# Attention, top-1 experts and a gated MLP on one core: gate values through TensorE, another order in the routing and in the first expert, four weight splits on GpSimd

## The chip, the cores and the metric

One core of a Trainium2 chip runs the whole program. The metric is the device time of one execution in microseconds (us); less is better. The engines are TensorE (PE; its weight loads are a row of their own, PEld), VectorE (DVE), ScalarE (ACT), GpSimd (POOL) and SyncE (SP). SP issues nearly all DMAs, POOL issues the DMAs that gather rows by index. Each engine works through its own queue in order and waits on semaphores.

## What is computed

Attention over 2 x 8 heads of 576 tokens and 64 columns, with the scores under (row maximum - tau) masked out; its output is a matrix `x` of 1152 rows and 512 columns. Each row goes to one of 8 experts:

```python
logits = x @ w_gate                       # 1152 x 8
expert_idx = np.argmax(logits, axis=1)
gate_w = softmax(logits)[arange, expert_idx]
h = relu(x_rows_of_e @ w1[e])             # 512 -> 1024
y = h @ w2[e]                             # 1024 -> 512
out[i] = gate_w[i] * y[row i]             # rows beyond the capacity: 0
# then: (silu(out @ w_gate2) * (out @ w_val)) @ w_out, 512 -> 1536 -> 512
```

## The kernel before

**Stages.** Attention runs to about 163 us, the routing to 174 us, the eight experts to about 300 us, the gated MLP to the end at 543 us. Work on the experts uses products in fp32r, in which each operand is a high part plus a low remainder; so each weight buffer is split in "pieces" of 128 x 1024: ScalarE writes the high part (`split_hi`, L220), VectorE subtracts it from the raw weights for the low part (L300). A ring of six pieces holds them. `next_piece` emits the split of the next piece; for VectorE the subtraction is put off to the call of `next_piece` that follows (`late`). `next_raw` lets SP load the next 1 MB of weights (four for each expert) when a raw buffer is free.

**Routing** (L1060 to L1230). From the logits VectorE makes a one-hot `oh`, the gate value `gs`, and counts `osb` for each partition. TensorE sums the counts over all partitions (`ps_c`), and makes each token's position inside its expert (prefix sums: `p0_` for the first expert, `pt_` for all). The experts are ordered by size: `key`, `krow` and `gc` come from the counts, and `pt_` is finished with `gc` (L1150). VectorE then derives the sorted place `dst` of each token, one-hot rows `olo`, and TensorE turns them into `ids`, the token of each sorted place. `info` holds the order of the experts, `slack` the number on which every engine branches to one of several programs; the one that runs here is the one for a smallest expert with at most 64 tokens ("packed").

**First expert.** Its rows are not gathered: `pick_rows` multiplies the rows by one-hot columns `hot` on TensorE (nine tiles of 128 tokens, eight short matmuls by two for each), and the sum `ps_x0` becomes `x0`.

**Other experts.** Every row of `x` lies in DRAM in `xd`, with its gate value as column 513 (`put_gates`, L1074: two DMAs of ScalarE, two of SP). POOL gathers the rows in sorted order, 128 to a tile (`gather`, L1290; the first three L1216). VectorE multiplies a tile by its gate column (`sort_scale`, L1304), TensorE transposes it (`sort_tile`, L1313, four matmuls), ScalarE copies it to `xsT` (L1322). `window(e)` takes an expert's columns out of `xsT`.

**Order.** All of this is a hand-written order of emission. `SORTP` is a table of ones and zeros: at which step of which expert a tile is sorted. `expert_first` runs the first expert: four products with `w1` (L1491), a turn of the result (`turn`, a fold on TensorE and two copies), four products with `w2`, and after each of these eight steps one call of `next_piece`. `expert_rows` does the same for the second and third (L1417, six matmuls a product).

Of the kernel before, what the change touches and what calls it, by code (L numbers as in the profile page):

```python
# [23 lines left out]
def attention_moe_swiglu_kernel(  # L24
# [35 lines left out]
    PK = 64  # L60
# [49 lines left out]
    AOLO = (5,)  # L110
    VH, PH, AH = (8,0), (1,2,3,4), (5,6,7)
# [15 lines left out]
    olo_all = const.tile([128, NTL, 128], F16, name="olo")  # L127
    olo = [olo_all[:, t] for t in range(NTL)]
    rhs = const.tile([128, NTL, NTL], F16, name="rhs")
    x0 = const.tile([128, KD, 2 * PK], F32R, name="x0")  # L130
# [146 lines left out]
    def next_piece(lo_eng=None, hi_eng=None):  # L277
        while late:
            late.pop()()
        if used["piece"] >= len(porder):  # L280
            return
# [3 lines left out]
        pr = ring[(used["piece"] + 2) % NRING]  # L285
        if nm in ("w1", "w2"):
# [782 lines left out]
    sqw = [rt_(f"sqw{i}", [128, 128], BF16) for i in range(len(AOLO))]  # L1069
# [4 lines left out]
    def put_gates():  # L1074
        gs = xr[NP - 1][:, :, 128]
        V.reciprocal(out=gs, in_=gsum)
        for b in range(B):
            nc.scalar.dma_start(
                xd[b * S:b * S + SM, DM:DM + 1].rearrange("(p c) d -> p (c d)", c=C4),
                gs[:, b * C4:(b + 1) * C4])  # L1080
            nc.sync.dma_start(xd[b * S + SM:(b + 1) * S, DM:DM + 1],
                              gs[b * ST:(b + 1) * ST, B * C4:NTL])

    def gate_ops():
        yield lambda: V.tensor_reduce(out=gsum, in_=pexp, axis=AX.X, op=ALU.add)
        yield lambda: V.tensor_scalar(out=gsum, in0=gsum, scalar1=1e-9, scalar2=None, op0=ALU.add)
        yield put_gates
# [23 lines left out]
    cols, rows_ = [(o0, ones), (o1, ones), (ot, ones)], [(ones, o0), (ones, o1), (ones, ot)]  # L1111
    for a, (l, r_) in enumerate(cols):
        mm(ps_c[0:NE, 0:1], l, r_[:, 0:1], start=a == 0, stop=a == 2)
    for a, (l, r_) in enumerate(rows_):
        mm(ps_c[0:NE, NE:2 * NE], l[:, 0:NE], r_, start=a == 0, stop=a == 2)
    pt_ = ps_r[:, 0:NTL * NE].rearrange("p (t e) -> p t e", t=NTL)
    M4 = B * C4

    p0_ = ps_c[:, 4 * NE:4 * NE + NTL]
    prefix = [(0, C4, upper, o0), (C4, NTL, ones, o0), (C4, M4, lowh, ot), (C4, M4, upper, o1),  # L1120
              (M4, NTL, upper, ot), (M4, NTL, highc, o1)]
    for i, (a, z, l, r_) in enumerate(prefix):
# [9 lines left out]
    mm(p0_[:, 0:M4], same, pre3[:, :, 0], start=False, stop=True)  # L1132
    for i, (a, z, l, r_) in enumerate(prefix):
        mm(pt_[:, a:z], l, r_.unsqueeze(1).to_broadcast([128, z - a, NE]), start=i == 0, stop=False)
    mm(pt_[:, 0:M4], same, pre3, start=False, stop=False)
    V.tensor_scalar(out=npos, in0=p0_, scalar1=-1.0, scalar2=None, op0=ALU.mult)

    def hot_v(t):
        V.tensor_scalar(out=hot[:, t], in0=iot[:, 0:PK], scalar1=npos[:, t:t + 1],
                        scalar2=gm[:, t:t + 1], op0=ALU.is_equal, op1=ALU.mult)  # L1140

    for t in VH[:1]:
        hot_v(t)
# [17 lines left out]
    hord = [VH[0], VH[1], PH[0], AH[0], PH[1], PH[2], AH[1], PH[3], AH[2]]  # L1161
# [11 lines left out]
    keep_warm(mp, WA[1])  # L1173
# [594 lines left out]
```

## Time and profile before

| | us |
|---|---|
| median of three runs | 545.84 (545.61 to 547.84) |
| the profiled execution | 544.49 |
| its span, first to last instruction | 542.7 |
| TensorE busy in the span | 525.4 (97%) |
| VectorE, ScalarE, GpSimd busy | 400.2, 296.6, 119.2 |

TensorE is the engine to read: from about 192 us to the end it has no gap, and its granted clock is at the full level (1.00) throughout. A row of the timeline gives start, duration, engine, line, operation, output and inputs, and in brackets the idle time before it with the instruction that ended it. TensorE's durations are modelled and overlap; the distance between two starts is the better measure.

### The profile page before, as it was taken

Reading aid. Unit: us, or ns where it says so; the run is one execution under the profiler, and the core shown is the slowest. Engines: PE = TensorE matmul, PEld = TensorE weight load, DVE = VectorE, ACT = ScalarE, POOL = GpSimd, SP = SyncE. Lnnn points to the kernel's source line nnn. Section 1 sums busy time; section 2 is a strip of 40 time slices with the busy share of each in tenths; the row PEclk is TensorE's granted clock in tenths of the full one; section 3 lists DMA queues with packets and bytes.
Section 4 is the critical chain, followed back from the end, with each engine's and each line's share of the span. In section 5 each row is a group of like instructions: output and inputs, shape, how many; then the busy total and the mean of one; then the engine's idle time right before and its main releaser. Section 6 shows DMA issues by size and latency. Waiting matters only on the chain. (4 is left out here: it accounts for less than half of the span.)

```text
span 542.7 us, 9898 instructions
## 1 busy us (share of the span) xinstructions
PE 525.4 (97%) x3648; PEld 474.2 (87%) x3648; DVE 400.2 (74%) x802; ACT 296.6 (55%) x571; POOL 119.2 (22%) x204
## 2 busy tenths in 40 slices
PE   7999999999998899999999999999999999999995
PEld 6778788888786588999999999999999999888884
DVE  6988989889966789988888968888885858622220
ACT  5986776767645699877777424234242224323221
POOL 6685292495644310000000000000000000021101
PEclk8999999999999999999999999999999999999999
DMA  6736256247303999866764442443431400001001
GB/s 190 219 93 137 71 118 131 70 97 209 124 18 74 391 398 352 308 226 231 241 197 133 146 150 81 152 134 101 155 115 46 153 2 0 1 39 40 35 24 44
DMA packets 63193, 73.83 MB, mean 136 GB/s; under 512 B 22432, under 2 KB 41504, under 8 KB 63136
## 3 DMA queue, kind: packets, MB, share of 16 engines
q1 hardware_dynamic: 60496, 68.38, 40.5%
q0 software_dynamic: 1440, 4.72, 2.2%
q8 instruction: 31, 0.51, 0.4%
q14 instruction: 26, 0.21, 0.1%
q10 hardware_dynamic: 1200, 0.00, 0.1%
HBM read 63.07 MB, written 4.72 MB: 125 GB/s over the span
## 5 line engine op out<-in xcount | busy, mean ns | idle before, releaser
L1668 PE MATMUL pgv<-yT,ring 128*128 128x384 f32 x828 | 145.3, 337 | 0.0
L1668 PEld LDWEIGHTS pgv<-yT,ring 128*128 128x128 f32 x828 | 145.1, 188 | 0.0
L1721 POOL DMA_INDIRECT out_dram<-ob,ids x9 | 10.1, 1119 | 319.1 <-ACT hs L220 270.1
L220 ACT CAST ring<-raw 128x1024 fp32r<-128x1024 f32 x48 | 51.2, 1069 | 50.2 <-DVE raw L248 48.4
L701 ACT COPY pT<-ps_pt 128x512 f32<-128x512 f32 (+1 forms) x108 | 52.3, 486 | 37.8 <-PE ps_pt L697 37.8
L675 DVE SCALAR_TENSOR_TENSOR e<-s,th,e 128x576 f32<-128x576 f32 x72 | 58.7, 815 | 5.5 <-ACT e L664 4.1
L651 DVE TENSOR_REDUCE nm<-s 128x1 f32<-128x576 f32 x72 | 54.2, 752 | 8.1 <-PE s L641 7.6
L664 ACT ACTIVATE e<-s,nm 128x576 f32<-128x576 f32 x72 | 54.3, 754 | 3.0 <-DVE nm L651 2.8
L224 DVE TENSOR_TENSOR hs<-h,hs 128x768 fp32r<-128x768 f32 x18 | 17.2, 958 | 48.1 <-ACT hs L220 48.1
L697 PE MATMUL ps_pt<-ident,e 128*128 128x128 f32 x324 | 46.9, 272 | 0.0
L220 ACT CAST ring<-rawx 128x1024 fp32r<-128x1024 f32 x28 | 29.4, 1055 | 26.0 <-DVE rawx L248 22.3
L1715 PE MATMUL po<-ring,hs 128*128 128x512 f32 x108 | 42.0, 389 | 0.0
L1716 PE MATMUL po<-ring,hs 128*128 128x512 f32 x108 | 42.0, 389 | 0.0
L1717 PE MATMUL po<-ring,hs 128*128 128x512 f32 x108 | 42.0, 389 | 0.0
L300 DVE TENSOR_TENSOR ring<-raw,ring 128x1024 fp32r<-128x1024 f32 x34 | 41.2, 1216 | 0.9 <-PE ps_h L1491 0.9
L1376 PE MATMUL ps_y<-h,ring 128*128 128x448 f32 (+3 forms) x144 | 41.5, 361 | 0.0
L719 PE MATMUL ps_pv<-pT,v 128*64 128x256 f32 (+2 forms) x400 | 40.4, 328 | 0.0
L697 PEld LDWEIGHTS ps_pt<-ident,e 128*128 128x128 f32 x324 | 39.0, 140 | 0.2 <-issue 0.2
L1377 PE MATMUL ps_y<-h,ring 128*128 128x224 f32 (+3 forms) x144 | 35.8, 248 | 0.0
L1688 ACT ACTIVATE sg<-pgv 128x384 f32<-128x384 f32 x36 | 17.6, 489 | 29.7 <-PE pgv L1668 17.8
L1689 DVE TENSOR_TENSOR h<-sg,pgv 128x384 f32<-128x384 f32 x36 | 19.6, 548 | 17.9 <-PE pgv L1668 17.5
L1376 PE MATMUL ps_h<-xw,ring 128*128 128x448 f32 (+3 forms) x112 | 32.6, 361 | 0.0
(289 smaller groups left out, 1079.8 us busy)
## 6 DMA issues: line engine op xcount, KB each, us to landing
raw<-in_moe_w_dram SPq DMA_DIRECT2D x20, 1024.0 KB, 6.0
rawx<-in_moe_w_dram SPq DMA_DIRECT2D x12, 1024.0 KB, 6.3
raw<-in_moe_w_gate_dram SPq DMA_DIRECT2D x6, 1024.0 KB, 5.8
raw<-in_moe_w_out_dram SPq DMA_DIRECT2D x5, 1024.0 KB, 4.8
raw<-in_moe_w_val_dram SPq DMA_DIRECT2D x3, 1024.0 KB, 5.1
rawx<-in_moe_w_val_dram SPq DMA_DIRECT2D x3, 1024.0 KB, 5.0
k<-in_k_dram SPq DMA_DIRECT2D x8, 256.0 KB, 3.7
q<-in_q_dram SPq DMA_DIRECT2D x8, 256.0 KB, 4.4
```

Source lines behind the costliest of these rows:

```text
L220: nc.scalar.copy(dst, src)
L300: lo_eng.tensor_tensor(out=lo_, in0=src, in1=f32(hi_), op=ALU.subtract)
L651: nc.vector.tensor_reduce(out=nm_t[u][:, j:j + 1], in_=s_t[i][:, :, 0:SH], axis=AX.XY, op=ALU.max, negate=True)
L664: nc.scalar.activation(out=e_t[u][:, j].rearrange("p (a s) -> p a s", a=2), in_=s_t[i][:, :, 0:SH], func=ACTF.Exp, bias=nm_t[u][:, j:j + 1 ...
L675: nc.vector.scalar_tensor_tensor(out=ev, in0=s_t.pop(i)[:, :, 0:SH], scalar=th_t[u][:, j:j + 1], in1=ev, op0=ALU.is_ge, op1=ALU.mult, accu ...
L697: nc.tensor.transpose(ps[:, c * 128:(c + 1) * 128], ef[:, (c0 + c) * 128:(c0 + c + 1) * 128], ident)
L701: return lambda: nc.scalar.copy(pT[g][:, c0:c0 + m, o:o + 128], ps[:, 0:m * 128].rearrange("p (c t) -> p c t", c=m))
L1376: mm(ps[:, 0:2 * W], ws(wp, 0), x[:, 0:2 * W], start=first, stop=False)
L1668: mm(ps[:, 0:TH], (gw, vw)[w][:, i, kk, fl * 128:(fl + 1) * 128], yT[:, x, kk, th * TH:(th + 1) * TH], start=i + x + kk == 0, stop=i == 1 ...
L1715: mm(po, hs[:, 0, fl], ws[:, 0, sl], start=f == 0, stop=False)
L1716: mm(po, hs[:, 0, fl], ws[:, 1, sl], start=False, stop=False)
L1717: mm(po, hs[:, 1, fl], ws[:, 0, sl], start=False, stop=f == KF2 - 1)
```

## The change

- **Gates.** `gs` stays in SBUF. The gate column of `xd`, and with it four DMAs, are dropped. Instead `gs` is split in three bfloat16 parts `gp`, multiplied into the one-hot `ohi` (`grhs`), and sorted with the same `olo` by nine more matmuls (`ps_gt`), whose sum is `gat`, the gate of each sorted place.
- **Keys ahead of prefix sums.** `key`, `krow`, `gc` come ahead of `npos` and the `hot` columns on VectorE; the prefix sums for the first expert move to another PSUM bank. The two filler matmuls ahead of `pick_rows` go.
- **`hot` and `olo`**: one `hot` column on VectorE instead of two, four on ScalarE instead of three; no `olo` on ScalarE. `ids` is made after six picked tiles, as before, but the gathers are emitted straight after it, two instead of three into the first buffer.
- **Gathers and scaling.** In the packed program a gather is emitted three tiles ahead. Tiles 2 to 8 are scaled by ScalarE. Clearing the end of `xsT` goes to POOL.
- **First expert, other order.** The subtraction of the fourth `w2` piece comes ahead of the low part of the first turn, two tiles (not three) are sorted in it, and it emits six pieces instead of eight; the other two follow in the second and third expert (`MORE`). `SORTP` sorts two tiles in each of the experts 1, 2 and 3 and one in expert 4.
- **GpSimd splits** (`POOLED`): both parts of the second and fourth `w2` piece of experts 1 and 2.

The core of the diff:

```diff
+    POOLED = tuple((e, "w2", g) for e in (1, 2) for g in (1, 3))
+    MORE = ((1, 3), (2, 3))
-    VH, PH, AH = (8,0), (1,2,3,4), (5,6,7)
+    VH, PH, AH = (8,), (0,1,2,3), (4,5,6,7)
...
+            if (e, nm, g) in POOLED and pooled:
+                lo_eng = hi_eng = nc.gpsimd
...
-    keep_warm(mp, WA[1])
     pick_rows(hord[:RT1])
...
     V.tensor_copy(out=ids, in_=ps_i[:, 0:NTL])
+    gbuf = idle.popleft()
+    first = [gbuf[:, t * DM:(t + 1) * DM] for t in range(2)]
+    for t in range(2):
+        nc.gpsimd.indirect_dma_start(first[t], None, xd[:, :],
+                                     bass.IndirectOffsetOnAxis(ap=ids[:, t:t + 1], axis=0))
+    pick_rows(hord[RT1:RT1 + 1])
...
+    V.tensor_tensor(out=gp[:, :, 0], in0=gs, in1=gs, op=ALU.max)
+    V.tensor_tensor(out=gm, in0=gs, in1=gp[:, :, 0], op=ALU.subtract)
+    V.tensor_tensor(out=gp[:, :, 1], in0=gm, in1=gm, op=ALU.max)
+    V.tensor_tensor(out=gp[:, :, 2], in0=gm, in1=gp[:, :, 1], op=ALU.subtract)
+    V.tensor_tensor(out=grhs, in0=ohi.unsqueeze(2).to_broadcast(TG),
+                    in1=gp.unsqueeze(3).to_broadcast(TG), op=ALU.mult)
...
+    for x, t in enumerate(tord):
+        mm(ps_gt[:, 0:3 * NTL], olo[t], grhs[:, t].rearrange("p v n -> p (v n)"), start=x == 0,
+           stop=x == NTL - 1)
...
+            if t < NTL and packed and t >= NG0:
+                nc.scalar.activation(out=grow[t], in_=grow[t], func=ACTF.Identity,
+                                     scale=gat[:, t:t + 1])
```

VectorE in the routing, after the counts `osb` and `pre` are made. In the changed kernel the small tiles of the routing are parts of two larger ones, so `npos` and `pos` read `spare_2453` and the `hot` columns `spare_2452`. Before:

```order
L1130 TENSOR_TENSOR pre<-pre,oh 128x2x8
L1136 TENSOR_SCALAR npos<-ps_c 128x9
L1139 TENSOR_SCALAR spare<-iot,npos,gm 128x64
L1144 TENSOR_SCALAR key<-ps_c,kcol 8x1
L1146 SCALAR_TENSOR_TENSOR krow<-ps_c,kadd 8x8
L1148 SCALAR_TENSOR_TENSOR gc<-krow,key,ps_c 8x8
L1139 TENSOR_SCALAR spare<-iot,npos,gm 128x64
L1175 TENSOR_TENSOR pos<-ps_r,oh 128x72
```

The same place in the changed kernel:

```order
L1132 TENSOR_TENSOR pre<-pre,spare_2453 128x2x8
L1140 TENSOR_SCALAR key<-ps_c,kcol 8x1
L1142 SCALAR_TENSOR_TENSOR krow<-ps_c,kadd 8x8
L1144 SCALAR_TENSOR_TENSOR gc<-krow,key,ps_c 8x8
L1157 TENSOR_SCALAR spare_2453<-ps_p 128x9
L1159 TENSOR_SCALAR spare_2452<-iot,spare_2453 128x64
L1183 TENSOR_TENSOR spare_2453<-ps_r,spare_2453 128x72
```

The three key instructions have moved ahead of `npos` and of the one `hot` column left, and `pos` follows that column.

VectorE again, from `ids` to the first instruction that follows the branch. Before:

```order
L1206 CAST ids<-ps_i 128x9
L1209 CAST info<-ps_c 3x8
L1210 TENSOR_TENSOR nd<-ps_c,wmax 1x24
L1212 TENSOR_REDUCE slack<-nd 1x3
L1226 TENSOR_TENSOR x_83<-ps_x_2549,x_83 128x2x64 x2
L1229 TENSOR_LOAD slack
```

The same place in the changed kernel:

```order
L1209 CAST ids<-ps_i 128x9
L1218 CAST info<-ps_c 3x8
L1219 TENSOR_TENSOR gp<-spare_2453 128x9
L1220 TENSOR_TENSOR spare_2453<-spare_2453,gp 128x9
L1221 TENSOR_TENSOR gp<-spare_2453 128x9
L1222 TENSOR_TENSOR gp<-spare_2453,gp 128x9
L1224 TENSOR_TENSOR grhs<-spare_2453,gp 128x243
L1226 TENSOR_TENSOR nd<-ps_c,wmax 1x24
L1228 TENSOR_REDUCE slack<-nd 1x3
L1240 TENSOR_TENSOR x_83<-ps_x_2537,x_83 128x2x64 x2
L1243 TENSOR_REDUCE gat<-ps_gt 128x9
L1245 TENSOR_LOAD slack
```

Five instructions for the gates now stand between `info` and `slack`.

POOL in the packed program, behind the branch, in the changed kernel (before, six gathers `g<-xd,ids` and nothing else stand there). The tiles `ring_97` to `ring_101` are slots of the ring of pieces, `raw` and `rawx` raw weights:

```order
L1377 MEMSET xsT 128x4x80
L1312 DMA g<-xd,ids 128x512 x4
L218 TENSOR_SCALAR ring_101<-rawx_2719 128x1024
L312 TENSOR_TENSOR ring_101<-rawx_2719,ring_101 128x1024
L218 TENSOR_SCALAR ring_97<-raw_103 128x1024
L312 TENSOR_TENSOR ring_97<-raw_103,ring_97 128x1024
L1312 DMA g<-xd,ids 128x512
L218 TENSOR_SCALAR ring_97<-rawx_2720 128x1024
L312 TENSOR_TENSOR ring_97<-rawx_2720,ring_97 128x1024
L1312 DMA g<-xd,ids 128x512
L218 TENSOR_SCALAR ring_99<-rawx_2719 128x1024
L312 TENSOR_TENSOR ring_99<-rawx_2719,ring_99 128x1024
```

Four splits of two instructions each have come in, with the last gathers between and behind them; those are the splits that ScalarE and VectorE no longer do.

## Rows read from the trace of the kernel before

**Rows 1.** Windows: busy us and instructions of PE, PEld, DVE, ACT, POOL; clock, DMA, GB/s
```profile
186.00:192.00 6.00, 4.71 (x25) 3.26 (x25) 4.84 (x7) 4.29 (x7) 0.00 (x0) 1.00 1.04 405
192.00:200.00 8.00, 8.00 (x43) 6.67 (x42) 6.97 (x9) 7.52 (x11) 0.94 (x1) 1.00 1.05 411
...
205.00:210.00 5.00, 5.00 (x27) 4.21 (x26) 5.00 (x7) 4.77 (x7) 0.94 (x1) 1.00 1.05 373
```

**Rows 2.** Timeline of TensorE from the routing to the second expert
```profile
167.29 0.44 PE L1150 MATMUL ps_r<-gc,onef 8*128 8x72 f32 x2 [0.93 <-DVE gc L1148]
167.66 0.60 PE L826 MATMUL ps_w<-masks 128*128 128x512 bf16 x2
...
171.21 0.38 PE L1205 MATMUL ps_i<-rhs,olo 128*128 128x9 f16 x9
...
174.41 3.00 PE L1491 MATMUL ps_h<-ring,x 128*128 128x512 f32 x12 [1.15 <-DVE x L1226]
177.30 1.10 PE L1499 MATMUL ps_ht<-pair,hb 128*128 128x64 f32 x8
178.21 1.17 PE L1491 MATMUL ps_h<-ring,x 128*128 128x512 f32 x4
...
184.39 0.66 PE L1313 MATMUL ps_g<-ident,raw 128*128 128x128 f32 x4 [1.10 <-DVE raw L1304]
184.81 2.10 PE L1491 MATMUL ps_y<-ring,ht 128*128 128x512 f32 x8
...
187.74 1.66 PE L1417 MATMUL ps_h<-ring,xw 128*128 128x512 f32 x6
190.52 1.10 PE L1499 MATMUL ps_yt<-pair,yb 128*128 128x64 f32 x8 [1.12 <-ACT yb L1504]
```

**Rows 3.** Timeline of VectorE in the routing
```profile
166.21 0.17 DVE L1136 TENSOR_SCALAR npos<-ps_c 128x9 f32<-128x9 f32 x1 [0.27 <-PE ps_c L1132]
...
167.02 0.21 DVE L1148 SCALAR_TENSOR_TENSOR gc<-krow,key,ps_c 8x8 f32<-8x8 f32 x1
...
167.76 0.23 DVE L1175 TENSOR_TENSOR pos<-ps_r,oh 128x72 f32<-128x72 f32 x1 [0.30 <-PE ps_r L1150]
...
171.63 0.17 DVE L1206 CAST ids<-ps_i 128x9 int32<-128x9 f32 x1 [0.74 <-PE ps_i L1205]
...
172.03 0.17 DVE L1212 TENSOR_REDUCE slack<-nd 1x3 int32<-1x24 f32 x1
```

**Rows 4.** The reads of slack, by queue, and VectorE's first instruction behind the branch
```profile
L1229 PEldq TENSOR_LOAD <-slack x1: 487/487/487, 172.5 to 172.5; - x1
...
L1229 DVEq TENSOR_LOAD <-slack x1: 555/555/555, 173.8 to 173.8; - x1
...
175.08 0.33 DVE L1357 MEMSET xsT<- 128x320 f32 x1 [0.82 <-issue]
```

**Rows 5.** The first gather: POOL's timeline, and us from issue to landing
```profile
172.43 1.21 POOL L1216 DMA_INDIRECT raw<-xd,ids  x1 [2.91 <-DVE slack L1212]
...
raw<-xd,ids POOLq DMA_INDIRECT x1, 5.9
```

**Rows 6.** Timeline of VectorE and of GpSimd at the program's start
```profile
6.26 0.29 DVE L387 TENSOR_SCALAR ring<-ring 128x256 fp32r<-128x256 f32 x1
6.47 0.77 DVE L387 TENSOR_SCALAR ktp<-kt 128x128 fp32r<-128x128 f32 x1
...
6.37 0.78 POOL L390 TENSOR_TENSOR ring<-q,ring 128x256 fp32r<-128x256 f32 x1 [0.43 <-ACT ring L404]
```

**Rows 7.** Groups by line and shape: count | busy us, mean ns | idle before
```profile
L300 DVE TENSOR_TENSOR ring<-raw,ring 128x1024 fp32r<-128x1024 f32 x34 | 41.2, 1216 | 0.9 <-PE ps_h L1491 0.9
L1304 DVE TENSOR_SCALAR g<-g 128x512 f32<-128x512 f32 x6 | 3.2, 533 | 0.0
...
L300 POOL TENSOR_TENSOR ring<-raw,ring 128x1024 fp32r<-128x1024 f32 x6 | 14.3, 2382 | 0.5
...
L218 POOL TENSOR_SCALAR ring<-raw 128x1024 fp32r<-128x1024 f32 x6 | 6.3, 1050 | 0.1
```

More of the change, by code (lines that the diff above doesn't have):

```diff
@@ L126, in attention_moe_swiglu_kernel @@
     upper, ones, lowh, highc, same = [masks[:, i] for i in range(5)]
[L127 to L128 removed]
     rhs = const.tile([128, NTL, NTL], F16, name="rhs")
+    gat = const.tile([128, NTL], F32, name="gat")
     x0 = const.tile([128, KD, 2 * PK], F32R, name="x0")
@@ L284, in next_piece @@
         nm, e, g = it
-        pr = ring[(used["piece"] + 2) % NRING]
+        slot = (used["piece"] + 2) % NRING
+        assert slots.get(slot) not in pieces, (it, slots[slot])
+        slots[slot] = it
+        pr = ring[slot]
         if nm in ("w1", "w2"):
@@ L1049, in attention_moe_swiglu_kernel @@
     R = {}
+    spare, room = [ep.tile([128, 2, S], F32, tag="e", name=f"spare{i}")[:, :, :].rearrange(
+        "p j s -> p (j s)") for i in range(2)]
+    taken = [0]
     def rt_(name, shape, dt=F32):
+        if shape[0] == 128 and dt == F32:
+            n = 1
+            for m in shape[1:]:
+                n *= m
+            t = room[:, taken[0]:taken[0] + n]
+            taken[0] += n
+            R[name] = t.rearrange("p (a b) -> p a b", a=shape[1]) if len(shape) == 3 else t
+            return R[name]
         R[name] = rp.tile(shape, dt, name=name)
@@ L1131, in attention_moe_swiglu_kernel @@
     pre3 = pre[:, :, :, :].rearrange("p b c e -> p (b c) e")
[L1132 to L1143, printed above, removed]
+    cols, rows_ = [(o0, ones), (o1, ones), (ot, ones)], [(ones, o0), (ones, o1), (ones, ot)]
+    for a, (l, r_) in enumerate(cols):
+        mm(ps_c[0:NE, 0:1], l, r_[:, 0:1], start=a == 0, stop=a == 2)
+    for a, (l, r_) in enumerate(rows_):
+        mm(ps_c[0:NE, NE:2 * NE], l[:, 0:NE], r_, start=a == 0, stop=a == 2)
+    cntc, cntr = ps_c[0:NE, 0:1], ps_c[0:NE, NE:2 * NE]
     V.tensor_scalar(out=key, in0=cntc, scalar1=float(NE), scalar2=kcol[:, 0:1], op0=ALU.mult,
@@ L1203, in attention_moe_swiglu_kernel @@
     ps_i = mp.tile([128, 512], F32, tag="m", name="ps_i")
+    ps_gt = mp.tile([128, 512], F32, tag="m", name="ps_gt")
     for x, t in enumerate(tord):
@@ L1239, in attention_moe_swiglu_kernel @@
     state = dict(used), dict(raws), dict(pieces)
-    idle0 = list(idle)
+    idle0, slots0 = list(idle), dict(slots)
     which0 = dict(which)
@@ L1251, in rest @@
         which.update(which0)
+        slots.clear()
+        slots.update(slots0)
+        pooled.clear()
         halves.clear()
@@ L1285, in rest @@
         offs_v, offs_a = {0: 0}, {0: 0}
-        grow = [gbuf[:, t * DX:(t + 1) * DX] for t in range(NG0)]
+        grow = list(first)
+        NG0 = len(first)
         def gather(g, t):
@@ L1354, in rest @@
             ev()
-        for t in range(NG0, NS0):
+        for t in range(NS0):
             gather_next(t + 3)
-        V.memset(xsT[:, :, NT:], 0.0)
+        nc.gpsimd.memset(xsT[:, :, NT:], 0.0)
         if not packed:
@@ L1603, in expert @@
                                hs[f], f == 0, f == KF - 1, last_y(e, m))
+                    if m == KD - 1:
+                        for i in range(4):
+                            pieces.pop(("w2", e, i))
                 else:
@@ L1621, in expert @@
                 elif e < NE - 1:
-                    next_piece()
+                    for _ in range(2 if packed and e in XE and m == 1 else 1):
+                        next_piece()
                 else:
```

170 lines of the change are left out of this document (86 added, 84 removed).

## The prediction

> **What bounds the kernel now.** First the windows and the timeline of TensorE. From about 192 us to the end TensorE stands in no gap, and in the windows around 186 to 210 us its busy time is the window's length at the full granted clock [rows 1]. So nothing behind 192 us can get shorter unless matmuls go, and none go there. What can be won are TensorE's waits and fillers before 192: 0.93 us for `gc`, two fillers, 1.15 for `x0`, 1.10 for a scaled tile, 1.12 for the copy of `yb` [rows 2], and the smaller waits inside the first expert. What can be lost is the supply of weight pieces in expert 1 and 2: between 186 and 210 us VectorE is busy for 4.84 of 6, 6.97 of 8 and 5.00 of 5 us, ScalarE for 7.52 of 8 in the middle window, and the 16 DMA engines for all of the time (share 1.04 to 1.05) [rows 1]. GpSimd is nearly idle there. The reader should keep these two apart: waits that end before 192, and a supply that is already close to full behind it.
>
> **Routing: -0.5 us.** The wait of 0.93 for `gc` [rows 2] is VectorE's queue: `gc` comes 0.81 behind `npos` (167.02 against 166.21), and `npos` and a `hot` column stand ahead of it [rows 3]. With the keys first `gc` is ready some 0.75 earlier; `pos`, which waits for the product with `gc`, goes from 167.76 to about 167.0. The fillers go, 0.53 by the distance of starts (167.66 to the 168.19 at which the first pick starts; the row's modelled 0.60 [rows 2] is the upper figure). So the picks, `ids` and `x0` come about 1.3 earlier: `ids` near 170.3 instead of 171.63 [rows 3]. A new product `ps_gt`, nine short matmuls, costs 0.4, by the nine of `ps_i` with 0.38 [rows 2].
>
> But the branch does not come 1.3 earlier. Between `ids` and `slack` now stand five instructions for the gates. Four have 128x9 values (0.17 each, by `npos` and `ids` [rows 3]) and one 128x243 (0.29, by the 128x256 at 6.26 [rows 6]): 0.97 together if nothing stalls, up to some 1.6 since each needs the one before it. So `slack` is written between 0.3 earlier and 0.3 later than at 172.03 [rows 3]. TensorE's queue reads it at about 172.5, VectorE's read came at 173.8, and VectorE's first instruction behind the branch started at 175.08, 1.28 after its read [rows 4]. If TensorE needs as much, the first product starts at 172.5 + 1.28 = 173.8, plus or minus 0.3, although `x0` is there by 173.1. Before it was 174.41 [rows 2]. I take 173.9: -0.5. The bounds: 173.1 (only `x0` counts, -1.3) and 174.4 (slack late, 0).
>
> The gathers are emitted behind `ids` and not behind the branch. The first one waited 2.91 until 172.43, for `slack`, and its rows took 5.9 to land [rows 5]. It can start near 171.1, so the first tile lands at about 177.0 instead of 178.3.
>
> **First expert: -2.3 us, and +0.4 later.** From the first product (174.41) to the first of expert 1 (187.74) it is 13.33 us [rows 2]. TensorE's own work in it: a product of four matmuls takes 0.96 (three in 177.30 - 174.41 = 2.89), eight are 7.7; two folds at 0.91 (178.21 - 177.30) are 1.8; each sorted tile costs 0.42 (184.81 - 184.39) [rows 2]. Before, with three tiles, that is 10.8, so 2.5 were waits; 1.10 of it was for one scaled tile [rows 2], whose scaling stood in VectorE's queue behind subtractions of 1.22 us [rows 7], not on its gather. Now ScalarE scales the later tiles, the tiles are gathered earlier, two are sorted here and not three, and two splits fewer are emitted. The work left is 7.7 + 1.8 + 0.8 = 10.3. One wait is new: the subtraction for the fourth `w2` piece stands ahead of the low part of the first turn, so the turn comes up to 1.22 later [rows 7]; the third and fourth products, which need no turn, cover part, and 0.55 is left (about the part of 1.22 beyond the 0.96 of a product, plus a semaphore's delay). With 0.15 for small waits: 11.0, so -2.3. Bounds: 10.25 (no wait) and 13.5 (the supply of weights sets the pace, as for the piece that came last before). The tile not sorted here is sorted later, where TensorE is full: +0.4.
>
> **Expert 1: -1.1 us.** The wait of 1.12 for `yb` [rows 2] was ScalarE's queue, where two splits stood around the copy; in the new order those are not there, so I take all of it. Bounds: 0 and -1.12.
>
> **GpSimd splits: +1.1 us.** Four splits move to GpSimd, 1.05 for the high part and 2.38 for the low part against VectorE's 1.22 [rows 7]: 4 x 3.43 = 13.7 us on an idle engine, in place of 4 x 1.05 on ScalarE and 4 x 1.22 on VectorE. They can start when their ring slots come free, behind expert 1's third product, and the last is needed by expert 2's last product: twelve products of six matmuls (6/4 x 0.96 = 1.45) and seven turns or tiles at 0.4 lie between, 20.2 us. Alone that fits by 6.5 us.
>
> The trace speaks against "alone". A 128x128 `TENSOR_SCALAR` on VectorE lasted 0.77 where one of twice the columns lasted 0.29; it ended within 0.1 us of the end of a GpSimd operation with two inputs in SBUF (6.37 + 0.78) [rows 6]. So VectorE was held up by GpSimd. If only one of the two runs at a time, GpSimd's 13.7 and VectorE's two-input work in the same stretch (seven subtractions of 1.22 and some copies for `xw`, 9.2) are 22.9 in 20.2: 2.7 short. Short operations that share lose less than their length, which takes the shortfall down to some 0.5. Bounds: 0, and 3.6 with the gaps between the operations. I take 1.1, nearer to the lower end since row 6's stall is at most one GpSimd operation. The relief on VectorE (5.00 of 5 [rows 1]) is counted in this.
>
> The Trainium skill, "SBUF — State Buffer", section "Who interferes with whom", states the rule: a VectorE instruction with two inputs in SBUF contends with a GpSimd instruction that reads SBUF, and whichever issues first keeps the port pair for its whole instruction. [rows 6] agrees for short ones, by the 0.77 against 0.29; no run here shows it for 128x1024. By it this term would be some 2.7 to 3.6, without it 0. It is the rival of the supply, below.
>
> **Edits at nothing.** The four gate DMAs: nothing that TensorE needs waits for them, as the gathers wait for `slack` [rows 5]. The memset of `xsT` (0.33 [rows 4]) leaves VectorE just behind the branch, where it had idled; on GpSimd it stands ahead of the gathers of tiles 2 and on, at most some 1 us each on those, which are needed 10 us later. The last three gathers stand behind splits on GpSimd's queue and wait for up to 3.43 us each; tiles 6 to 8 are sorted in expert 3 and 4. If that cover went, one sort would wait some 3 us. ScalarE gets seven scalings (at VectorE's 0.533 [rows 7]), 3.7 us over four experts, and gives up 4.2 of casts: nothing.
>
> **Sum.** -0.5 - 2.3 + 0.4 - 1.1 + 1.1 = -2.4. The profiled execution had 544.49, which becomes 542.1. It lies 1.35 below the median of 545.84; the same difference on the median gives **543.4**.
>
> **The rivals.**
> - *No stall on the port*: -3.5, so 542.3; with the best routing (-1.3) 541.5. For it: GpSimd has 6.5 us of room, and its six splits of this shape before took the undisturbed 2382 and 1050 [rows 7]. Against it: [rows 6].
> - *The supply sets the pace*: VectorE and GpSimd take turns for the 128x1024 splits (+3.6 in place of +1.1), or the weights themselves do (DMA share of 1.04 to 1.05 [rows 1]), so that what is won ahead is waited for again. Then -2.4 + 2.5 = +0.1, or 545.9; with the weights alone, where only the routing's part and a little is kept, 545.
> - *VectorE stands still for all of GpSimd's splits*: the slower side. While GpSimd runs a split, no subtraction runs; TensorE consumes the pieces at its own rate, so the pieces that VectorE owes come late by GpSimd's 13.7 less the 4 x 1.22 that it is spared: 8.8. Then -3.5 + 8.8 = +5.3, or 551.1. It decides from a stall over 3.5 on, and shows as slower by more than 0.5% from 6.2 on. Against it: VectorE's queue runs some products ahead, and the splits are spread over 20 us.
> - *The change doesn't do what it says in expert 0*: the tiles land early, but what the sort waited for was VectorE's queue, and the new order only moves the queue to ScalarE. Then -1 of the -2.3 stays: 544.7, inside the forecast's range.
>
> **Chances.** A measurement can tell about 0.5%, 2.7 us, so faster means below 543.1 and slower over 548.6. Forecast 0.47, with its own range 542.4 to 544.9, of which 0.17 lies below 543.1; no stall 0.26, all faster; supply 0.18, of which 0.17 the same and 0.01 slower; standing still 0.09, of which 0.07 slower. That gives faster 0.43, same 0.49, slower 0.08. The range of 541.3 to 546.2 holds the first three cases and leaves out the fourth and the ends of the others.
>
> **What would show it.** First product of expert 0 at about 173.9; later than 174.4 means the gate instructions ahead of `slack` are on the path. First product of expert 1 at about 185.0 (174.41 - 0.5 + 11.0); no wait ahead of its first fold of `yb`. VectorE's subtractions during GpSimd's splits: 1.22 means no lock, over 2 means they hold each other up. A gap of TensorE before a product in expert 1 or 2 that ends on a piece made by GpSimd or VectorE is the +1.1; none there is the first rival; over 3.5 us of them is the third. Wrong altogether would be a gap behind expert 2, which none of these cases has.

## The result: no gain, 0.3 to 0.5% slower

The changed kernel took 549.15 us (median of 7 runs, 547.13 to 549.28) against 545.84 for the kernel before; the ratio is 1.0051 (95% interval 1.003 to 1.0072). Measured again beside the experiments it took 547.34 against 546.21, ratio 1.0030 (1.0014 to 1.0046). The forecast was 543.4, faster by 2.4.

The times of either kernel spread over 2 us and more. For the changed kernel two profiles show where most of it lies: 549.28 and 547.28 us, and attention ends 1.68 us later in the slower one, whose matmuls from 13 to 17 us take longer (granted clock 0.50 in that stretch, against 1.00 in the other). The same four matmuls in the kernel before, in the changed kernel, and in the changed kernel once more (e1_same):

```profile
12.80 0.78 PE L641 MATMUL s<-kp,ring 128*128 128x288 f32 x4 [0.70 <-DVE th L659]
```
```profile
13.33 1.30 PE L653 MATMUL s<-kp,ring 128*128 128x288 f32 x4 [0.70 <-DVE th L671]
```
```profile
13.29 0.77 PE L653 MATMUL s<-kp,ring 128*128 128x288 f32 x4 [1.05 <-DVE th L671]
```

The change has no line there. So all comparisons of stages below start at the fillers at the end of attention (matmuls `ps_w<-masks`, whose result nothing uses), which come behind this, and end at TensorE's last matmul. By this measure the changed kernel gave 376.24 and 376.21 us in its two profiles, though their spans are 547.2 and 545.1.

Every other kernel has one profile, so its stages are those of one execution. The one of the kernel before lies 1.35 us under that kernel's median, and by this measure the best version below is 4.4 us ahead of it, by the medians 5.2. Differences against the kernel before may thus be off by about 1 us; the changed kernel is 2.35 behind it in the trace, and 1.1 and 3.3 by the two pairs of medians.

### The profile page after: what moved, and what is told of

Read it like the earlier page. It is cut to its first block, busy times and chain, and to the rows that moved or that the text cites. A ratio compares the mean times of both kernels' runs of the same rounds, so it can differ in the third digit from the quotient of the medians.

```text
span 547.2 us, 9914 instructions
## 1 busy us (share of the span) xinstructions
PE 527.9 (96%) x3654; PEld 476.5 (87%) x3655; DVE 403.5 (74%) x795; ACT 297.5 (54%) x575; POOL 135.9 (25%) x213
## 3 DMA queue, kind: packets, MB, share of 16 engines
q0 software_dynamic: 1440, 4.72, 2.3%
HBM read 63.06 MB, written 4.72 MB: 124 GB/s over the span
## 5 line engine op out<-in xcount | busy, mean ns | idle before, releaser
L1762 POOL DMA_INDIRECT out_dram<-ob,ids x9 | 8.8, 975 | 313.4 <-ACT ob L1761 306.2
L220 ACT CAST ring<-raw 128x1024 fp32r<-128x1024 f32 x47 | 49.7, 1067 | 50.4 <-DVE raw L248 48.5
L312 DVE TENSOR_TENSOR ring<-raw,ring 128x1024 fp32r<-128x1024 f32 x33 | 47.0, 1441 | 4.7 <-PE ps_h L1519 2.4
L709 PE MATMUL ps_pt<-ident,e 128*128 128x128 f32 x324 | 48.0, 276 | 0.0
L220 ACT CAST ring<-rawx 128x1024 fp32r<-128x1024 f32 x25 | 26.4, 1055 | 22.4 <-DVE rawx L248 22.3
```

The costliest lines, as they stand in the source:

```text
L220: nc.scalar.copy(dst, src)
L312: lo_eng.tensor_tensor(out=lo_, in0=src, in1=f32(hi_), op=ALU.subtract)
L709: nc.tensor.transpose(ps[:, c * 128:(c + 1) * 128], ef[:, (c0 + c) * 128:(c0 + c + 1) * 128], ident)
```

## The profile after

TensorE's timeline in the changed kernel: the fillers, the first product of expert 0 (175.84), 1 (186.85) and 3 (218.65), all waits of 0.3 us and more between, and the last matmul.

```profile
164.93 2.75 PE L838 MATMUL ps_w<-masks 128*128 128x512 bf16 x11
...
174.62 0.39 PE L1231 MATMUL ps_gt<-grhs,spare 128*128 128x27 bf16 x9 [0.43 <-DVE grhs L1224]
175.84 3.00 PE L1519 MATMUL ps_h<-ring,x 128*128 128x512 f32 x12 [0.83 <-DVE gat L1243]
...
181.26 1.20 PE L1519 MATMUL ps_y<-ring,ht 128*128 128x512 f32 x4 [0.45 <-DVE ht L1542]
...
186.85 1.57 PE L1443 MATMUL ps_h<-ring,xw 128*128 128x512 f32 x6
...
196.95 2.57 PE L1443 MATMUL ps_y<-ring,ht 128*128 128x512 f32 x10 [0.32 <-POOL ring L312]
...
201.72 1.19 PE L1443 MATMUL ps_y<-ring,ht 128*128 128x512 f32 x4 [1.30 <-POOL ring L312]
...
209.25 1.20 PE L1443 MATMUL ps_h<-ring,xw 128*128 128x512 f32 x4 [0.40 <-DVE ring L312]
...
212.41 1.33 PE L1443 MATMUL ps_y<-ring,ht 128*128 128x512 f32 x4 [1.51 <-DVE ring L312]
...
218.65 0.38 PE L1396 MATMUL ps_h<-xw,ring 128*128 128x288 f32 x1
...
230.61 0.40 PE L1396 MATMUL ps_y<-h,ring 128*128 128x288 f32 x1 [0.81 <-DVE h L1598]
...
248.92 0.43 PE L1396 MATMUL ps_y<-h,ring 128*128 128x352 f32 x1 [0.49 <-DVE h L1598]
...
541.17 0.39 PE L1758 MATMUL po<-ring,hs 128*128 128x512 f32 x1
```

The same marks of the kernel before that [rows 2] don't have: the fillers, the first product of expert 2 and of expert 3, the last matmul.

```profile
162.84 2.75 PE L826 MATMUL ps_w<-masks 128*128 128x512 bf16 x12
...
202.95 1.55 PE L1417 MATMUL ps_h<-ring,xw 128*128 128x512 f32 x6
...
216.20 0.29 PE L1376 MATMUL ps_h<-xw,ring 128*128 128x288 f32 x1
...
536.73 0.39 PE L1717 MATMUL po<-ring,hs 128*128 128x512 f32 x1
```

The differences of these starts give the time by stage. The experiments (e2 and on) stand in the same table, each explained below.

| us | fillers to expert 0 | expert 0 | expert 1 | expert 2 | expert 3 to the last matmul | sum |
|---|---|---|---|---|---|---|
| before | 11.57 | 13.33 | 15.21 | 13.25 | 320.53 | 373.89 |
| changed | 10.91 | 11.01 | 15.90 | 15.90 | 322.52 | 376.24 |
| e2: no GpSimd splits | 10.90 | 11.02 | 14.04 | 14.16 | 322.51 | 372.63 |
| e3: high part on GpSimd | 10.90 | 11.02 | 14.21 | 14.33 | 322.50 | 372.96 |
| e13: low part on GpSimd | 10.92 | 10.98 | 13.98 | 14.86 | 322.76 | 373.50 |
| e9: GpSimd splits, VectorE scales | 10.91 | 11.01 | 15.89 | 16.56 | 322.12 | 376.49 |
| e8: none, VectorE scales | 10.91 | 10.99 | 13.82 | 13.33 | 321.80 | 370.85 |
| e11: none, GpSimd scales | 10.91 | 11.10 | 13.69 | 13.32 | 320.77 | 369.79 |
| e12: as e8, gates on GpSimd | 10.49 | 11.02 | 13.80 | 13.31 | 321.84 | 370.46 |
| e14: e11 and e12 | 10.50 | 11.00 | 13.85 | 13.32 | 320.84 | 369.51 |

So routing and expert 0 gained 0.66 and 2.32, as forecast. Expert 1 and 2 gave 0.69 and 2.65 back, and 1.99 went behind them, where only the 0.4 of a tile was forecast. In expert 1 and 2 TensorE had four waits for pieces, 3.53 us: two for pieces that GpSimd made (0.32 and 1.30), two for VectorE's (0.40 and 1.51). What held the pieces up is seen on VectorE and GpSimd between 193 and 216 us. VectorE's subtractions in that stretch:

```profile
194.58 3.39 DVE L312 TENSOR_TENSOR ring<-raw,ring 128x1024 fp32r<-128x1024 f32 x1 [0.26 <-ACT ring L220]
...
199.36 9.84 DVE L312 TENSOR_TENSOR ring<-raw,ring 128x1024 fp32r<-128x1024 f32 x4
...
209.72 2.64 DVE L312 TENSOR_TENSOR ring<-rawx,ring 128x1024 fp32r<-128x1024 f32 x1
...
212.88 2.81 DVE L312 TENSOR_TENSOR ring<-rawx,ring 128x1024 fp32r<-128x1024 f32 x1
```

GpSimd's splits (the last one, at 210 to 215 us, is left out):

```profile
193.34 1.08 POOL L218 TENSOR_SCALAR ring<-rawx 128x1024 fp32r<-128x1024 f32 x1
194.50 2.39 POOL L312 TENSOR_TENSOR ring<-rawx,ring 128x1024 fp32r<-128x1024 f32 x1
196.86 2.04 POOL L218 TENSOR_SCALAR ring<-raw 128x1024 fp32r<-128x1024 f32 x1
198.98 2.68 POOL L312 TENSOR_TENSOR ring<-raw,ring 128x1024 fp32r<-128x1024 f32 x1
...
204.87 3.24 POOL L312 TENSOR_TENSOR ring<-rawx,ring 128x1024 fp32r<-128x1024 f32 x1
```

The subtraction at 194.58 began 0.08 behind GpSimd's and ended at 197.97, 1.08 behind the latter's end at 196.89: it waited for all of it, and then took nearly its usual 1.22. GpSimd's next copy (196.86) took 2.04 instead of 1.05 [rows 7]: now it had to wait for VectorE. They take turns. Over the stretch the seven subtractions of VectorE took 18.68 us, where seven at 1.22 are 8.54: it lost 10.1 us, and was spared four subtractions, 4.9. GpSimd lost too: its second piece took 2.04 + 2.68 = 4.72 instead of 3.43, as much more as TensorE waited for it (1.30). The windows that answer to [rows 1] show GpSimd's side of it, the columns as there:

```profile
186.00:192.00 6.00, 6.00 (x34) 4.98 (x33) 4.81 (x7) 5.12 (x8) 0.11 (x1) 1.00 1.03 381
192.00:200.00 8.00, 7.68 (x40) 6.08 (x39) 6.61 (x6) 5.99 (x10) 7.81 (x5) 1.00 1.00 369
205.00:210.00 5.00, 4.60 (x24) 3.56 (x23) 5.00 (x4) 4.16 (x7) 3.97 (x2) 1.00 0.94 354
```

GpSimd is busy for 7.81 of 8 us, and VectorE, about as busy as before, finishes fewer instructions (6 instead of 9, 4 instead of 7). The Trainium skill, "SBUF — State Buffer", section "Who interferes with whom", says that a VectorE instruction with two inputs in SBUF contends with a GpSimd instruction that reads SBUF; these rows agree for 128x1024, which no run had shown ahead of the change.

## Experiments

The text of each expectation names a theory, its rivals, and the time that each would give.

**e1_same: the changed kernel again.**

> The changed kernel, unaltered. In its first profile TensorE reached the end of attention 2.1 us later than in the kernel before, and its granted clock fell to 0.50 in 10 to 15 us, where the kernel before had 0.80; no line of that stretch is changed. Theory port (GpSimd's splits hold up VectorE's subtractions): the attention's end varies from run to run, between about 162.8 and 165 us, and has nothing to do with the change; the waits of TensorE for pieces in expert 1 and 2 come again, 3.5 us in sum within 0.7. Rival start (the loss lies ahead of the routing and belongs to the changed kernel): attention ends at 164.9 again, and every time is 547 to 549.5.

Attention ended at 163.25 instead of 164.93; the waits for pieces came again (0.33, 1.30, 0.41, 1.49). The start varies without the change, the loss in expert 1 and 2 doesn't.

**e2_no_pool: without the GpSimd splits.**

```diff
-    POOLED = tuple((e, "w2", g) for e in (1, 2) for g in (1, 3))
+    POOLED = ()
```

> The changed kernel without its four GpSimd splits: ScalarE and VectorE do them as all others. Theory port: the waits for pieces in expert 1 and 2 (0.32, 1.30, 0.40, 1.51) and the two for the h of VectorE behind them (0.81, 0.49) go, 4.8 us: 544.3 within 0.8, and VectorE's subtractions are 1.22 throughout. Rival start: what costs lies ahead of the routing, so at most 2.5 us come back: 547 or more. Rival stock (two splits were put off from expert 0 to expert 1 and 2, so that fewer pieces are ready there, whoever makes them): the waits stay, and with VectorE and ScalarE fuller they grow: 549 to 552.

543.92 us, ratio 0.9963 (0.9946 to 0.9981). Expert 1 and 2 are 1.86 and 1.74 shorter, the sum 3.61, and the mean subtraction is 1.22. Three waits of TensorE are left behind expert 0:

```profile
204.11 0.66 PE L1452 MATMUL ps_ht<-ident,hb 128*128 128x128 f32 x4 [0.40 <-ACT hb L1462]
...
225.02 0.40 PE L1396 MATMUL ps_y<-h,ring 128*128 128x288 f32 x1 [0.82 <-DVE h L1598]
...
243.33 0.43 PE L1396 MATMUL ps_y<-h,ring 128*128 128x352 f32 x1 [0.45 <-DVE h L1598]
```

So the theory holds for the pieces in expert 1 and 2, but not for the 1.3 in expert 3 and 4, which it had been expected to take along.

**e3_pool_high_only and e13_pool_low_only: one of GpSimd's two operations.**

```diff
-                lo_eng = hi_eng = nc.gpsimd
+                hi_eng = nc.gpsimd
```

In e13 it is `lo_eng` that is set.

> The changed kernel with GpSimd making only the high part of the four pieces (a one-input operation of 1.05 us alone), the subtractions are VectorE's again. Theory port, if only GpSimd operations with two inputs hold VectorE up: subtractions of 1.22, no waits, as without GpSimd: 544.3. Theory port, if every GpSimd operation that reads the buffers does: subtractions that meet one last up to 1.05 longer, at most 4.2 us of VectorE's time, of which a third or so reaches TensorE: 545.5. Rival start: 547 or more. Rival stock: 549 or more.

> The changed kernel with GpSimd making only the low part (two inputs) of the four pieces; ScalarE makes their high part. From the last fillers to TensorE's last matmul the changed kernel has 376.2, without GpSimd splits 372.6, with the high part alone on GpSimd 373.0. Theory two inputs (the subtraction on GpSimd is what holds VectorE up, and the copies for the high part hardly do): 375.5 to 376.5. Rival sum (it is GpSimd's whole time of 3.43 us for a piece, one part after the other, that makes the pieces late): 373.5 to 374.5, since each piece is ready 1 us earlier and GpSimd is busy for 9.5 instead of 13.7 us.

In the trace the high part alone costs 0.33 (372.96, 544.13 us), the low part alone 0.87 (373.50, 546.35 us), both 3.61. So it isn't the low part as such (the theory of e13), and the two parts don't add up to the whole: with both, GpSimd is busy without a break from 193.34 to 201.66, so that VectorE meets one operation after the other. The times say this less clearly: against e2 the medians are 0.2 higher in e3, 2.4 in e13 and 3.4 in the changed kernel, and e13's profile is the fastest of its ten executions. VectorE was held up in either: in e3 the subtraction at 192.56 lasted 2.06 beside a copy from 192.48 to 193.54. GpSimd's and then VectorE's rows of e13:

```profile
191.96 2.41 POOL L312 TENSOR_TENSOR ring<-rawx,ring 128x1024 fp32r<-128x1024 f32 x1 [0.53 <-ACT ring L220]
194.82 2.90 POOL L312 TENSOR_TENSOR ring<-raw,ring 128x1024 fp32r<-128x1024 f32 x1 [0.45 <-ACT ring L220]
```
```profile
193.34 2.11 DVE L312 TENSOR_TENSOR ring<-raw,ring 128x1024 fp32r<-128x1024 f32 x1 [0.25 <-ACT ring L220]
...
196.09 2.18 DVE L1392 TENSOR_TENSOR xw<-xsT,xw 128x512 fp32r<-128x512 f32 x1
```

Here GpSimd waits 0.53 and 0.45 for ScalarE ahead of its subtractions; the pauses fall to VectorE, which is spared four subtractions besides. In e13 no wait of TensorE for a piece reaches 0.3 us any more; what it waits for in expert 2 are two copies of ScalarE (0.39 and 0.40).

**e4_before_plus_pool: only the GpSimd splits, in the kernel before.**

> The kernel before with the four GpSimd splits as the only change. Theory port: VectorE's subtractions that meet them last 2.4 to 3.4 instead of 1.22, TensorE waits some 3.5 to 5 us in expert 1 to 4: 549 to 551. Rival start: 545.8. Rival stock: here no split is put off, so there are pieces in stock and the waits are short: 545 to 547.

552.28 us, ratio 1.0102 (1.0072 to 1.0132). Expert 1 and 2 took 16.79 and 18.14, 6.5 us more than before; one wait of TensorE was 3.02, for the low part of a turn on VectorE. (Its profile, at 553.46, lost another 1.5 in the routing, where eight rows of picks took 0.60 to 0.69 instead of 0.40 to 0.45 at a granted clock of 0.66 from 167 to 172 us, and 1.0 in expert 0; so the time of that execution overstates the splits.) No split is put off here, so the rival "stock" is out.

**e6_eight_pieces: the two splits put off come back to expert 0 (no GpSimd splits).**

```diff
-    MORE = ((1, 3), (2, 3))
+    MORE = ()
...
-                if n != 2:
-                    next_piece()
+                next_piece()
...
                 if n == 1:
                     sort_now()
+                    next_piece()
```

> No GpSimd splits, and the first expert emits eight pieces as before the change, so that expert 2 and 3 have none put off to them. Without GpSimd splits TensorE still waits 0.40 in expert 2 and 1.27 in expert 3 and 4 for VectorE's h. Theory debt (those waits are the two splits put off): they go, expert 0 gets some of it back through VectorE's fuller queue: expert 0 from 11.0 to between 11.0 and 12.3, sum 543.0 to 544.0. Rival scaling (they come from ScalarE's tile scalings): they stay, and expert 0 gets longer: 544.3 to 545.5.

546.31 us. The waits behind expert 2 fell from 1.3 to 0.49, so part of them was that debt; but the way to expert 1's first product took 13.82, since that product waited 2.64 for `xw`, which stood behind two more subtractions in VectorE's queue. These waited in their turn for ScalarE's copies, and the first of the copies for weights that had not landed (1.36). Behind the wait the granted clock was 0.60 from 188 to 191 us, and expert 1 took 15.52. The sum is 375.34: putting the two splits off is worth 2.7 us in the trace, 2.4 by the medians. Neither the theory's times nor the rival's came out.

**e8_scaling_on_vector: VectorE scales all tiles (no GpSimd splits).**

```diff
-            if t < NTL and packed and t >= NG0:
+            if False:
                 nc.scalar.activation(out=grow[t], in_=grow[t], func=ACTF.Identity,
```

> No GpSimd splits, and VectorE scales all nine tiles, as before the change. Theory debt (VectorE is late in expert 2 to 4 by the splits put off): seven scalings of 0.48 more, 3.4 us, make its waits longer: 544.5 to 546. Rival scaling (ScalarE's scalings delay the hb copy and h): the waits of 0.40 and 1.27 go, 542.5.

541.63 us, ratio 0.9919 (0.9893 to 0.9945), 1.78 less in the trace than e2, though VectorE got 3.4 us more to do. ScalarE's scaling takes longer than the 0.533 at which it was priced [rows 7], and in ScalarE's queue it stands ahead of the copies `hb` that TensorE waits for (the 0.40 above, gone in e8). The two waits for `h` shrank to 0.31 and 0.25; by which way ScalarE's scaling reaches `h`, which VectorE writes, was not followed. The group in the changed kernel:

```profile
L1322 ACT ACTIVATE g<-g,gat 128x512 f32<-128x512 f32 x7 | 5.1, 733 | 0.0
```

**e9_pool_and_vector_scaling: the same with the GpSimd splits kept.**

> The changed kernel with its GpSimd splits, but VectorE scales all nine tiles. From the last fillers to TensorE's last matmul it is 376.2 us in the changed kernel, 372.6 without GpSimd splits, 370.9 without these and with VectorE's scaling. Theory two causes (the splits cost 3.6 by holding VectorE up, ScalarE's scaling costs 1.8 by delaying what TensorE waits for, each for itself): 376.2 - 1.8 = 374.4, time 545.5. Rival one resource (VectorE's time is what lacks in both; 3.4 us of scaling on a VectorE that is held up make it worse): 377 or more, time 548.

547.58 us, 376.49 in the trace, near the rival's 377 and far from 374.4: the 1.78 were not to be had while GpSimd's splits ran. Beside ScalarE's scaling the splits cost 3.61, beside VectorE's 5.64 (e9 against e8). This fits the rival: under the splits VectorE's time is what lacks, and its scalings take from it (expert 2: 16.56).

**e11_scaling_on_gpsimd: GpSimd scales tiles 2 to 8 (no splits on it).**

```diff
+                (nc.gpsimd if packed and t >= NG0 else V).tensor_scalar(
+                    out=grow[t], in0=grow[t], scalar1=gat[:, t:t + 1], scalar2=1.0, op0=ALU.mult,
+                    op1=ALU.mult)
```

> No GpSimd splits, tiles 2 to 8 scaled by GpSimd: seven one-input operations of about 0.6 us each, 128x512. Theory port: VectorE's subtractions that meet one last up to 0.6 longer, at most 4.2 in sum, against 3.4 that VectorE saves: 370.9 from the last fillers to the last matmul within 0.7, no gain from an idle engine. Rival free engine (only long two-input splits hurt): the last wait of 0.31 for VectorE's h goes, 370.4 or less, and no subtraction over 1.3. The gathers behind a scaling on GpSimd's queue may come late: a wait for a tile would show that.

541.06 us, ratio 0.9921 (0.9895 to 0.9947), 1.06 less in the trace than e8: the last waits for `h` are gone, and the mean subtraction stays at 1.23. By their times e8, e11, e12 and e14 can't be told apart (the intervals of the ratios overlap); what is said of their order rests on one trace each. This time it is GpSimd that waits. Three of its seven scalings, the first beside no VectorE instruction with two inputs in SBUF, the others beside subtractions in a row:

```profile
191.55 0.71 POOL L1325 TENSOR_SCALAR g<-g,gat 128x512 f32<-128x512 f32 x1
...
199.78 1.81 POOL L1325 TENSOR_SCALAR g<-g,gat 128x512 f32<-128x512 f32 x1
...
206.47 2.69 POOL L1325 TENSOR_SCALAR g<-g,gat 128x512 f32<-128x512 f32 x1
```

**e5_gates_before_info and e12_gates_on_gpsimd: `slack` earlier.** In e5 the five gate instructions move ahead of `info`; in e12 GpSimd makes the three parts while it waits for `ids`, and only `grhs` stays on VectorE, behind `slack` (e5 over e2, e12 over e8).

```diff
+    nc.gpsimd.tensor_scalar(out=gp[:, :, 0], in0=gs, scalar1=1.0, scalar2=1.0, op0=ALU.mult, op1=ALU.mult)
+    nc.gpsimd.tensor_tensor(out=gm, in0=gs, in1=gp[:, :, 0], op=ALU.subtract)
...
     V.tensor_copy(out=info[0:3], in_=rr)
-    V.tensor_tensor(out=gp[:, :, 0], in0=gs, in1=gs, op=ALU.max)
...
     V.tensor_reduce(out=slack[0:1], in_=nd, axis=AX.X, op=ALU.max)
+    V.tensor_tensor(out=grhs, in0=ohi.unsqueeze(2).to_broadcast(TG),
```

> No GpSimd splits (as the second run), and the five gate instructions on VectorE moved ahead of the copy of info, where VectorE had waited 0.57 us for TensorE. In the changed kernel slack was written at 174.84 and the first product of expert 0 started 1.00 later, while its rows x0 were there 0.6 earlier. Theory gates (the gate instructions ahead of slack are on the path): slack comes 0.5 to 0.6 earlier against the picks, and so does the product: 10.90 from the last fillers to it become 10.3 to 10.4, and the time 543.4. Rival rows (x0 sets the start): 10.9 stay, 543.9.

> No GpSimd splits, VectorE's scaling, the three gate parts made by GpSimd while it waits for ids, and their product with the one-hot on VectorE behind slack instead of ahead of it; info is not moved. Theory gates: slack comes 1.0 to 1.2 earlier, the first product of expert 0 starts 10.3 to 10.5 behind the last fillers instead of 10.9, and since the load of weights that waits for info is not put off (that was so in the fifth run, where expert 0 got 0.9 longer), expert 0 stays within 0.2 of 11.0: 370.4, time 541.2. Rival weights (the landing of weights sets expert 0's pace, so that an earlier start only waits): expert 0 gets as much longer as it starts earlier, 370.9.

In both the first product came 0.4 earlier (10.51, 10.49), though `slack` was written 0.65 and 1.26 earlier against the fillers: from there on `x0` sets the start, the rival of e5. In e12 the product came at 173.51, 0.24 behind the end of `x0`:

```profile
172.78 0.49 DVE L1240 TENSOR_TENSOR x<-ps_x,x 128x128 fp32r<-128x128 f32 x2 [0.79 <-ACT x L1237]
```
```profile
173.51 3.00 PE L1519 MATMUL ps_h<-ring,x 128*128 128x512 f32 x12 [0.92 <-DVE gat L1243]
```

In e5 expert 0 then took 11.90 and expert 1 14.61, a loss of 1.04 in the sum (373.67, 545.62 us): `info` came 0.6 later, and with it SP's load of the next weights; ScalarE waited 1.18 for these weights at 180.54. In e12 `info` stays, and the gain too: 541.28 us, ratio 0.9914 (0.9895 to 0.9934).

**e7_late_gathers and e10_gathers_behind_branch: the first gathers late.** In e7 they were only written behind `slack` in the code; they still started with `ids`, 7.95 behind the fillers, and nothing changed (expert 0 11.02, sum 372.62 against 372.63 in e2), so that it decides nothing between theory and rival. In e10 they stand behind the branch.

> No GpSimd splits, and the first two gathers are emitted behind slack, as before the change. Theory queue (the sorted tile of expert 0 waited for VectorE's queue, not for its rows): the gathers start 1.6 to 2 later, tile 0 lands later than 178 but ahead of its scaling at 181.1, expert 0 stays at 11.0: 543.9. Rival gathers: expert 0 goes to 12 to 13: 545 to 546.

> No GpSimd splits, VectorE's scaling, and the first two gathers emitted behind the branch, so that they can't start ahead of slack (in the seventh run they still started with ids). They start about 2.5 us later. Theory queue (expert 0's sorted tiles wait for VectorE's queue): tile 0 lands 2.5 later, at about 15.5 behind the last fillers, ahead of its scaling at 16.2; expert 0 stays at 11.0. Rival gathers: expert 0 gets 1 to 2.5 longer.

In e10 the first started 11.74 behind the fillers, 3.8 later than in the changed kernel and 2.2 later than before the change, and expert 0 took 16.43. VectorE's scaling, TensorE's rows, and the window behind the wait (columns as in [rows 1]):

```profile
183.72 0.62 DVE L1322 TENSOR_SCALAR raw<-raw,gat 128x512 f32<-128x512 f32 x1 [2.62 <-DMA raw<-xd,ids]
```
```profile
184.40 1.11 PE L1330 MATMUL ps_g<-ident,raw 128*128 128x128 f32 x4 [2.05 <-DVE raw L1322]
...
186.87 2.05 PE L1518 MATMUL ps_y<-ring,ht 128*128 128x512 f32 x4
```
```profile
184.00:188.00 4.00, 3.60 (x15) 3.41 (x16) 2.29 (x4) 1.43 (x3) 0.10 (x1) 0.54 1.04 390
```

The rows took some 7 us to land, where the changed kernel's took 5.0; and after a wait of 2.05 TensorE went on slower, nearly all of it at the lower of its two clocks, 1.2 GHz (granted 0.54 from 184 to 188 us): four matmuls took 2.05 where they take 1.2. So expert 0 lost 5.4, more than the rival had said, and not all of it is the rows. In the changed kernel the first tile landed at about 177.9 (172.88 + 5.0) and was scaled at 181.12, so some 3 us are to spare: by these rows the queue set the time there, as the theory has it, and a start 3.8 us later, with a longer landing, is more than it can bear. Whether the start in the kernel before (9.59) would do in the new order was not tried.

**e14_combined: e11 and e12 together.**

> No GpSimd splits; GpSimd scales tiles 2 to 8 (as in the eleventh run, 369.8 from the last fillers to the last matmul) and makes the three gate parts (as in the twelfth, where the first product started 0.42 earlier). Theory (each for itself): 369.4, time 540.6. Rival weights (expert 0 gives the earlier start back): 369.8.

540.78 us, ratio 0.9905 (0.9882 to 0.9928); 369.51 in the trace. Of the gains of e11 and e12 over e8, 1.45 in sum, 1.34 are there: they nearly add up. It is the best version here, 0.95% ahead of the kernel before: the change without its GpSimd splits, with GpSimd in the place of ScalarE for the scalings.

## Why the prediction was wrong

The likeliest case, -2.4, came out as +2.35 in the trace. Two terms of the sum failed: the GpSimd splits, put at +1.1, cost 3.61, and ScalarE's scalings, put at nothing, cost 1.78. A third loss, behind expert 2, was ruled out. By its steps:

- **Routing, -0.5:** -0.66, right by what sets the start: the first product came 1.00 behind the end of `slack`, and 0.60 behind that of `x0`. The number is in part luck, as two errors met. `slack` came 0.55 later against the fillers than before, more than the 0.3 allowed: `info` waited 0.57 for a matmul that now stands behind another picked tile, which the working had not seen, and the gate instructions took 1.24 from the first to `nd`. Against that, the way from the end of `slack` to the product was 1.00, where the working had 1.6 (172.20 to 173.8). VectorE's rows in the changed kernel, and TensorE's read of `slack`:

```profile
172.41 0.17 DVE L1209 CAST ids<-ps_i 128x9 int32<-128x9 f32 x1
173.14 0.15 DVE L1218 CAST info<-ps_c 3x8 int32<-3x8 f32 x1 [0.57 <-PE ps_c L1216]
173.23 0.15 DVE L1219 TENSOR_TENSOR gp<-spare 128x9 bf16<-128x9 f32 x1
...
174.47 0.16 DVE L1226 TENSOR_TENSOR nd<-ps_c,wmax 1x24 f32<-1x24 f32 x1
174.67 0.17 DVE L1228 TENSOR_REDUCE slack<-nd 1x3 int32<-1x24 f32 x1
174.77 0.47 DVE L1240 TENSOR_TENSOR x<-ps_x,x 128x128 fp32r<-128x128 f32 x2
```
```profile
L1245 PEldq TENSOR_LOAD <-slack x1: 489/489/489, 174.9 to 174.9; - x1
```

- **Expert 0, -2.3:** -2.32, right; the new wait was 0.45 where 0.55 was taken. That it hangs on the two splits fewer is shown by e6, where expert 0 took 13.82 with all eight; the share of the earlier gathers is open.
- **Expert 1, -1.1:** without the GpSimd splits and ScalarE's scalings -1.39 (e8), of which 1.12 is the wait for `yb` [rows 2]. Right, and 0.27 beyond its bound. (The reading of [rows 1] ahead of it isn't: from 186 to 192 us TensorE was busy for 4.71 of 6 us, this wait among the rest, so its busy time is the window's length only from 192 on.)
- **GpSimd splits, +1.1:** the term that failed most. It is +3.61 (e2), the upper bound of the range given, 3.6. The mechanism was named, and the rows between 193 and 216 us show it; its size was taken by the nearest row instead of by the sum. [rows 6] is one VectorE instruction, with one input, that meets one short GpSimd operation; so it was no case of the rule for two inputs that the prediction reads it as. Here GpSimd had two long operations for each piece without a pause, and VectorE's queue had no pause either: in such a stretch the two engines' times add, as the sum of 22.9 us in 20.2 said, and the 2.7 us by which that sum was short were not too many, as the prediction held, but fewer than the measured 3.61. By the traces of e3 and e13 the reasoning by parts ("short ones lose less") holds where GpSimd pauses. VectorE did lose 10.1 of GpSimd's 13.7, 5.2 more than it was spared; that TensorE lost 3.61 and not the rival's 8.8 fits what was said against that rival, the pieces ahead and the spread over 20 us.
- **Scalings on ScalarE, at nothing:** +1.78 (e8 against e2), 0.22 in expert 1, 0.83 in expert 2, 0.71 behind. They were weighed as busy time, 3.7 us in and 4.2 out. It was 5.1. That the place in the queue counted, ahead of copies that TensorE waits for, is shown by rows for the 0.40 in expert 2 only.
- **The tile put off, +0.4, and nothing behind expert 2:** with neither GpSimd splits nor ScalarE's scaling (e8) the stretch from expert 3 on is 1.27 longer than before, one tile 0.36 and waits for `h`, 0.6 on TensorE's row and 1.2 on that of its weight loads; with VectorE relieved as well (e11) it is 0.24. The two splits put off are part of it: with them back in expert 0 (e6) the waits for `h` fell from 1.27 to 0.49. The prediction had ruled this out: "Wrong altogether would be a gap behind expert 2".

The rivals: "no stall" fell with the rows above, "standing still" with the size. Together: -0.66 - 2.34 - 1.39 + 0.08 (expert 2) + 1.27 (e8), + 1.78 + 3.61 = +2.35. The case that the supply sets the pace, by turns of VectorE and GpSimd, is what happened to the pieces; it had +0.1 from the splits' full price, and lacked the scaling and the loss behind expert 2.

## What to carry to other kernels

Work moved to an idle GpSimd beside a VectorE that subtracts from SBUF all the time is not moved to free time: add both engines' times, and take what they exceed the stretch by as the price, not as the bound (here 2.7, and 3.61 measured). Short one-input operations with pauses between them (e11) cost TensorE nothing here, and 13.7 us of long ones with hardly a pause cost 3.61. Price a moved operation by its place in the new queue and by who waits behind it, not by its length; and follow what hangs on each instruction that a new one is put in front of (here `info`, and with it a weight load).

## What had not been expected of the hardware

- Which of the two engines waits is not the same in all pairs: beside GpSimd's 128x1024 splits VectorE's subtractions took up to 3.39 in the rows above instead of 1.22; beside GpSimd's 128x512 scalings they stayed at 1.23, and GpSimd took up to 2.69 instead of 0.71. The Trainium skill, "SBUF — State Buffer", section "Who interferes with whom", has the rule that the one which issues first gets the shared port for its whole instruction. It doesn't tell that: 2.69 is 1.98 more than 0.71, and one subtraction is 1.22. Why is open; the two GpSimd operations also differ in size, output type and operand form.
- The granted clock recorded for 13 to 17 us was 0.50 in the changed kernel's first profile and 1.00 in e7's, while the same matmuls took 1.30 in both, against 0.78 in the kernel before. That the matmuls ran at the lower level in e7 too is inferred from the equal durations; the recorded clock doesn't show it.
